# Strassen's seven products for the first expert product of four batches, with its sums on GpSimd

## The chip, the cores and the metric

The kernel runs on one core of a Trainium2 chip. The metric is the device time of one execution in microseconds (us), as the median of several runs. The engines are TensorE (PE, matrix products; its weight loads are listed as PEld), VectorE (DVE), ScalarE (ACT), GpSimd (POOL) and SyncE (SP, which here issues loads). Each engine has its own list of instructions and works it off in order; semaphores hold an instruction until what it needs is there. SBUF is the on-chip memory, PSUM the eight banks that TensorE writes; one bank holds 128 x 512 fp32 values.

## The reference

What is computed, cut to what matters here. A cross-attention between `x` (8 batches, 8 heads, 512 tokens of 64) and 32 states a head gives 4352 rows of 512; then each row goes to the one expert of eight that its gate picks.

```python
scores = scale * np.matmul(x, state.transpose(0, 1, 3, 2))      # softmax -> a
xread  = np.matmul(a, state)                                    # 512 rows per batch
scores2 = scale * np.matmul(state, x.transpose(0, 1, 3, 2))     # softmax -> a2
sread  = np.matmul(a2, x)                                       # 32 rows per batch
x = concatenate([xread, sread], axis=2) -> (B*S, H*D)           # 4352 x 512
logits = x @ w_gate                                             # 8 experts
for e in range(E):
    mask = argmax(logits, 1) == e
    h  = np.maximum(x[mask] @ w1[e], 0.0)                       # 512 -> 1024
    out[mask] = gate_w[mask, None] * (h @ w2[e])                # 1024 -> 512
```

The kernel does not form `xread` for the 512 token rows of a batch. As `xread = a @ state`, it multiplies the states with `w1` once (`G`, 256 x 1024) and then takes `h = relu(G^T a)`, with an inner length of 256 in place of 512. Everything is fp32.

## The kernel before

Per batch b the main part runs two products, both on TensorE. `up` is the first: eight blocks of 128 hidden units, each two matmuls of 128 x 128 by 512 columns into one bank, then a relu on ScalarE into `hT`.

```python
def new_hT():
    return [ffn.tile([128, S], FP32, tag="hT", bufs=NFC, name="hT") for _ in range(NFC)]   # NFC = 8

def up(G, a, hT, i=ALL, insert=None, every=2):
    n = i.stop - i.start
    for f in range(NFC):
        ph = bank("ph")[:, 0:128 * n]
        for g in range(2):
            pe.matmul(ph, lhsT=G[:, g, ts(f, 128)], rhs=a[:, i, g, :], start=(g == 0), stop=(g == 1))
        relu(hT[f][:]..., ph...)
        if insert and f % every == every - 1:
            next(insert, None)                 # a slot: other work is put in here
    return hT
```

The second product is plain (`down`) for batches 0 to 2. For batches 3 to 7 it already goes by Strassen's halves in Winograd's form: seven products of halves in place of eight. The products are named `pX`, `pD`, `pX` again (added onto the first), `pY`, `pZ`, `pW`, `pD` again; each is eight matmuls of 256 columns. The sums of activations (`Sa`, `Sb`) are made on VectorE, those of weights (`Ta`, `Tb`) on GpSimd, and results are combined in `yh` by VectorE.

```python
def down_by_halves(b, hT, w2t, insert, between):
    ...
    Sa, Sb, Ta, Tb = (new(t) for t in ("Sa", "Sb", "Ta", "Tb"))
    for f in range(4):
        dve.tensor_tensor(Sa[:, f], A(1, 0, f), A(1, 1, f), ALU.add)
    gp.tensor_tensor(Ta[:], W(0, 1), W(0, 0), ALU.subtract)
    ...
    pX = new_bank("pX")
    product(pX, lambda f: A(0, 0, f), W(0, 0))
    ...
    done()                                     # between(n), a slot, between(n) again
    pD = new_bank("pD")
    product(pD, lambda f: Sa[:, f], Ta)
    ... (pX again, pY, pZ, pW: as above)
    product(pD, lambda f: Sa[:, f], W(1, 1), start=False)
    store(yB, 1, 0)
    add(yA, pD, yA, 0)
    store(yA, 0, 1)                            # stores are issued by ScalarE
    done()
```

Between the products 3 and 4 the next batch's `G` is made (`pG`, copied out by ScalarE). Into the slots goes first the attention of later batches, then the rounds: the state rows (256 in all) are sorted by expert into groups of 32, four groups a round, three rounds. One round is `ptx` (transposes), four jobs `pgh` (a quarter of the first product), `pth` (transposes), four jobs `pgy` (a quarter of the second). Its weights come in tiles `s` of 1 MB, each as four loads, four tiles for the first product and three for the second. A `yield` ends the work of one slot; two in a row leave a slot empty.

```python
def rounds(r0, r1):
    ...
    round_experts(r0)
    fetch(2, 0)
    yield
    yield
    round_in(r0)                               # load of xg
    fetch(S1B - 2, S2B)
    for _ in range(6):
        yield
    for r in range(r0, r1):
        round_x(r)                             # ptx
        ...
        for k in range(NDC):
            round_up(r, k)                     # pgh
            fetch(2, 0)
            yield
            if k < NDC - 1 and r + 1 < r1:
                yield
        round_relu(r)
        yield
        round_h(r)                             # pth
        yield
        for f in range(0, NFC, 2):
            for i in range(2):
                round_down(r, f + i)           # pgy
                fetch(0, 1)
            if f + 2 == NFC:
                round_out(r)
            yield
            if r + 1 < r1:
                yield
```

The first product of batch b + 1 follows the second of batch b. PSUM has four banks in turn for all these products, two more (`t`) for `ptx`, `pth` and `pG`, and two (`g`) for `pgh` and `pgy`.

Of the kernel before, what the change touches and what calls it, by code (L numbers as in the profile page):

```python
# [9 lines left out]
FP32 = mybir.dt.float32  # L10
# [3 lines left out]
ALU = mybir.AluOpType  # L14
# [6 lines left out]
def kernel(  # L21
# [34 lines left out]
    B, H, S, D = x.shape  # L56
# [497 lines left out]
    def relu(dst, src):  # L554
        act.activation(dst, src, AF.Relu)
# [14 lines left out]
        return G  # L570

    def new_hT():
        return [ffn.tile([128, S], FP32, tag="hT", bufs=NFC, name="hT") for _ in range(NFC)]

    def up(G, a, hT, i=ALL, insert=None, every=2):

        n = i.stop - i.start
        for f in range(NFC):
            ph = bank("ph")[:, 0:128 * n]
            for g in range(2):  # L580
                pe.matmul(ph, lhsT=G[:, g, ts(f, 128)], rhs=a[:, i, g, :], start=(g == 0), stop=(g == 1))
            relu(hT[f][:].rearrange("p (c i t) -> p i c t", c=NC, i=4)[:, i],
                 ph.rearrange("p (i c t) -> p i c t", i=n, c=NC))
            if insert and f % every == every - 1:
                next(insert, None)
        return hT

    def down(hT, w2t, store, insert=None, between=None):
        for c in range(NC):
            py = bank("py")  # L590
            for f in range(NFC):
                pe.matmul(py[:], lhsT=hT[f][:, ts(c, 128)], rhs=w2t[:, f, :],
                          start=(f == 0), stop=(f == NFC - 1))
                if insert and f == 3:
                    next(insert, None)
            store(c, py)
            if insert:
                step = between(c)
                next(step)
                next(insert, None)  # L600
                next(step)

    def down_by_halves(b, hT, w2t, insert, between):


        def A(i, j, f):
            return hT[4 * j + f][:, ts(i, 256)]

        def W(j, k):
            return w2t[:, ts(j, 4), ts(k, 256)]  # L610

        def new(tag):
            return late["sst"].tile([128, 4, 256], FP32, tag=tag, name=tag)

        Sa, Sb, Ta, Tb = (new(t) for t in ("Sa", "Sb", "Ta", "Tb"))
        for f in range(4):
            dve.tensor_tensor(Sa[:, f], A(1, 0, f), A(1, 1, f), ALU.add)
        gp.tensor_tensor(Ta[:], W(0, 1), W(0, 0), ALU.subtract)
        for f in range(4):
            dve.tensor_tensor(Sb[:, f], A(0, 0, f), A(1, 0, f), ALU.subtract)  # L620
        gp.tensor_tensor(Tb[:], W(1, 1), W(0, 1), ALU.subtract)
        g = [gw[:, NC * b + c, :] for c in range(NC)]
        rows = out[ds(b * SO, S)].rearrange("(p c) f -> p c f", c=NC)
        n = [0]

        def product(to, a, w, start=True, stop=True):
            for c in range(2):
                for f in range(4):
                    pe.matmul(to[:, c], lhsT=a(f)[:, ts(c, 128)], rhs=w[:, f], start=(start and c == f == 0),
                              stop=(stop and f == 3), skip_group_check=True)  # L630
            n[0] += 1

        def done():
            step = between(n[0])
            next(step)
            next(insert, None)
            next(step)

        def new_bank(name):
            return bank(name)[:].rearrange("p (c d) -> p c d", c=2)  # L640

        def new_y():
            return ffn.tile([128, 2, 256], FP32, tag="y", bufs=YB, name="yh")

        def store(y, i, k):
            no_dep(act.dma_start(out=rows[:, ts(i, 2), ts(k, 256)], in_=y[:]))

        def add(y, p, u, i):
            for c in range(2):
                dve.scalar_tensor_tensor(y[:, c], p[:, c], g[2 * i + c], u[:, c], ALU.mult, ALU.add)  # L650

        pX = new_bank("pX")
        product(pX, lambda f: A(0, 0, f), W(0, 0))
        yA, yB = new_y(), new_y()
        for i, y in enumerate((yA, yB)):
            for c in range(2):
                act.activation(y[:, c], pX[:, c], AF.Copy, scale=g[2 * i + c])
        done()
        pD = new_bank("pD")
        product(pD, lambda f: Sa[:, f], Ta)  # L660
        for f in range(4):
            dve.tensor_tensor(Sa[:, f], Sa[:, f], A(0, 0, f), ALU.subtract)
        gp.tensor_tensor(Ta[:], W(1, 1), Ta[:], ALU.subtract)
        done()
        product(pX, lambda f: A(0, 1, f), W(1, 0), start=False)
        yC = new_y()
        for c in range(2):
            act.activation(yC[:, c], pX[:, c], AF.Copy, scale=g[c])
        store(yC, 0, 0)
        done()  # L670
        pY = new_bank("pY")
        product(pY, lambda f: Sa[:, f], Ta)
        add(yA, pY, yA, 0)
        add(yB, pY, yB, 1)
        for f in range(4):
            dve.tensor_tensor(Sa[:, f], A(0, 1, f), Sa[:, f], ALU.subtract)
        gp.tensor_tensor(Ta[:], W(1, 0), Ta[:], ALU.subtract)
        done()
        pZ = new_bank("pZ")
        product(pZ, lambda f: Sb[:, f], Tb)  # L680
        add(yB, pZ, yB, 1)
        yD = new_y()
        add(yD, pD, yB, 1)
        done()
        pW = new_bank("pW")
        product(pW, lambda f: A(1, 1, f), Ta)
        store(yD, 1, 1)
        add(yB, pW, yB, 1)
# [4 lines that stand above are left out]
        store(yA, 0, 1)  # L693
        done()
# [175 lines left out]
    def rounds(r0, r1):  # L870
        need1.extend((r, k, half) for r in range(r0, r1) for k in range(NDC) for half in range(2))
        need2.extend((r, f) for r in range(r0, r1) for f in range(NFC))
# [3 lines that stand above are left out]
        yield  # L876
        round_in(r0)
        fetch(S1B - 2, S2B)
        for _ in range(6):
            yield  # L880
        for r in range(r0, r1):
            round_x(r)
            if r + 1 < r1:
                round_experts(r + 1)
                round_in(r + 1)
            yield
            for k in range(NDC):
                round_up(r, k)
# [6 lines that stand above are left out]
            round_h(r)  # L895
# [3 lines that stand above are left out]
                    round_down(r, f + i)  # L899
                    fetch(0, 1)  # L900
                if f + 2 == NFC:
                    round_out(r)
                yield
                if r + 1 < r1:
                    yield


    early, lazy = [], []
    begin()

    def first():
# [45 lines left out]
    def batch(b):  # L957

        nonlocal G, hT

        def between(c):
            nonlocal G
            if c == (1 if b else 2) and b + 1 < B:
                G = states_w1(new_G(), w1s[b + 1], stG[:, b + 1])
            yield
            if c == 1 and 0 < b < B - 2:
                lazy.extend(w1_parts(b + 2, expert_of(eb, b + 2)))
            yield

        def between_products(n):  # L970
            nonlocal G
            if n in (3, 4) and b + 1 < B:
                if n == 3:
                    G = new_G()
                states_w1(G, w1s[b + 1], stG[:, b + 1], (n - 3,),
                          lambda name: late["ps_t"].tile([128, 512], FP32, tag="t", bufs=2, name=name))
            yield
            if n == 4 and b + 2 < B:
                lazy.extend(w1_parts(b + 2, expert_of(eb, b + 2)))
            yield  # L980

        if b < NE:
            down(hT, w2s[b], store_batch(b), slots, between)
        else:
            down_by_halves(b, hT, w2s[b], slots, between_products)
        if 0 < b < B - 2:
            lazy.extend(w2_parts(b + 2, expert_of(eb, b + 2)))
        if b + 1 < B:
            hT = up(G, aT[b + 1], new_hT(), insert=slots)
        if b == 0:  # L990
            e2 = expert_of(eb, 2)
            lazy.extend(w1_parts(2, e2) + w2_parts(2, e2))
# [126 lines left out]
```

## Time and profile before

| | before |
|---|---|
| median of three runs | 463.08 us (462.61 to 463.59) |
| span of the profiled execution | 460.7 us |
| DMA, whole span | 110.04 MB, mean 239 GB/s |
| first product of the batch 4, 5 or 6 (`ph` x32 with its slots) | from 245.5, 296.8 and 347.7 us |

The profile is one execution. In its slices, groups and chain every instruction is named by engine, operation and tile, for instance `ph<-aTl,G` for a matmul that reads `aTl` and `G` and writes `ph`. Each fp32 matmul appears as two records. Nearly all instructions stand at line L48, which is a helper that records them, so one goes by the tiles' names. The attention and batches 0 to 2 fill the time to about 200 us; batch 3's first product follows from 199.9 us, and from there on each batch takes about 51 us.

### The profile page before, as it was taken

Reading aid. Unit: us, or ns where it says so; the run is one execution under the profiler, and the core shown is the slowest. Engines: PE = TensorE matmul, PEld = TensorE weight load, DVE = VectorE, ACT = ScalarE, POOL = GpSimd, SP = SyncE. Lnnn points to the kernel's source line nnn. Section 1 sums busy time; section 2 is a strip of 40 time slices with the busy share of each in tenths; the row PEclk is TensorE's granted clock in tenths of the full one; section 3 lists DMA queues with packets and bytes.
Section 4 is the critical chain, followed back from the end, with each engine's and each line's share of the span. In section 5 each row is a group of like instructions: output and inputs, shape, how many; then the busy total and the mean of one; then the engine's idle time right before and its main releaser. Section 6 shows DMA issues by size and latency. Waiting matters only on the chain.

```text
span 460.7 us, 9525 instructions
## 1 busy us (share of the span) xinstructions
PE 442.5 (96%) x3713; PEld 252.7 (55%) x3713; DVE 177.4 (39%) x445; ACT 119.2 (26%) x266; POOL 87.7 (19%) x76
## 2 busy tenths in 40 slices
PE   3899999999999999999999999999999999999995
PEld 3575545454545544446674475636674466636652
DVE  4838662738275552233240224104131215102231
ACT  1333233533323433223212231022203220123100
POOL 2011040322121230023322022031331022400300
PEclk9999999999999999999999999999999999999999
DMA  6980588315675632539999976999869986690492
GB/s 194 340 283 2 179 272 295 124 55 183 249 221 213 213 112 98 167 90 346 377 306 381 384 285 206 328 340 402 290 203 365 390 284 208 243 334 30 123 367 72
DMA packets 68402, 110.04 MB, mean 239 GB/s; under 512 B 12927, under 2 KB 27263, under 8 KB 68352
## 3 DMA queue, kind: packets, MB, share of 16 engines
q1 hardware_dynamic: 60096, 99.86, 63.7%
q10 hardware_dynamic: 7856, 8.47, 5.2%
q0 software_dynamic: 400, 1.05, 0.6%
q8 instruction: 31, 0.51, 0.5%
q14 instruction: 19, 0.16, 0.1%
HBM read 94.15 MB, written 14.95 MB: 237 GB/s over the span
## 4 chain that ended last, share of the span: by engine, by line
PE 82%; DVE 10%; DMA 3%; ACT 2%; issue 1%; SPq 1%; POOL 1%; ACTq 0%; POOLq 0%; DVEq 0%
PE ph L48 20%; PE py L48 12%; PE pD L48 8%; PE pX L48 8%; PE pgy L48 5%; PE pgh L48 5%; PE pW L48 4%; PE pY L48 4%; PE pZ L48 4%; PE pc L48 4%; PE pG L48 3%; DVE xt L48 3%; DVE sm L48 1%; PE pt L48 1%; DVE nm L48 1%; DMA w1t<-in_moe_w_dram 1%
## 5 line engine op out<-in xcount | busy, mean ns | idle before, releaser
L48 PE MATMUL py<-w2t,hT 128*128 128x512 f32 x192 | 87.5, 601 | 0.0
L48 PE MATMUL ph<-aTl,G 128*128 128x512 f32 x160 | 71.6, 599 | 0.0
L48 ACT ACTIVATE hT<-ph 128x512 f32<-128x512 f32 (+1 forms) x72 | 39.2, 550 | 123.2 <-PE ph L48 123.0
L48 PEld LDWEIGHTS py<-w2t,hT 128*128 128x128 f32 x192 | 34.7, 190 | 39.2 <-issue 38.7
L48 PEld LDWEIGHTS ph<-aTl,G 128*128 128x128 f32 x160 | 29.4, 190 | 40.1 <-issue 39.2
L48 POOL TENSOR_TENSOR Ta<-w2t,Ta 128x1024 f32<-128x1024 f32 x10 | 24.9, 2486 | 135.1 <-PE pD L48 99.2
L48 PE MATMUL ph<-aTe,G 128*128 128x256 f32 (+1 forms) x128 | 44.0, 493 | 0.5 <-DVE aTe L48 0.5
L48 PE MATMUL pX<-w2t,hT 128*128 128x256 f32 x160 | 36.4, 380 | 0.0
L48 PEld LDWEIGHTS pX<-w2t,hT 128*128 128x128 f32 x160 | 30.0, 190 | 6.4 <-issue 2.6
L48 PEld LDWEIGHTS ph<-aTe,G 128*128 128x128 f32 x128 | 23.3, 190 | 15.7 <-issue 12.9
L48 DVE TENSOR_TENSOR Sa<-hT 128x256 f32<-128x256 f32 x20 | 9.7, 503 | 49.3 <-ACT hT L48 49.3
L48 DVE SCALAR_TENSOR_TENSOR yh<-pY,gw,yh 128x256 f32<-128x256 f32 x20 | 8.3, 476 | 45.5 <-PE pY L48 45.5
L48 PE MATMUL pgy<-s,shT 128*32 128x512 f32 x192 | 25.6, 599 | 0.0
L48 ACT ACTIVATE yh<-pX,gw 128x256 f32<-128x256 f32 x30 | 12.0, 473 | 44.7 <-PE pX L48 41.8
L48 POOL TENSOR_TENSOR sx<-sx,mx 128x1024 f32<-128x1024 f32 x6 | 11.5, 1912 | 63.5 <-DVE mx L48 63.5
L48 PE MATMUL pgh<-s,sxT 128*32 128x512 f32 x192 | 23.1, 598 | 0.0
L48 ACT COPY G<-pG 128x512 f32<-128x512 f32 x32 | 16.8, 593 | 24.3 <-PE pG L48 24.3
L48 PE MATMUL pc<-xt,stT 32*32 32x128 f32 x1024 | 18.3, 295 | 3.9 <-DVE xt L48 3.9
L48 DVE STREAM_TRANSPOSE sx<-pc 128x256 f32<-128x256 f32 x32 | 11.6, 418 | 23.8 <-PE pc L48 23.8
L48 PE MATMUL pG<-w1t,stG 64*32 64x512 f32 x256 | 19.0, 605 | 1.1 <-DMA w1t<-in_moe_w_dram 1.1
L48 ACT ACTIVATE y<-py,gw 128x512 f32<-128x512 f32 x12 | 8.3, 688 | 44.3 <-PE py L48 44.3
L48 PE MATMUL pW<-Ta,hT 128*128 128x256 f32 x80 | 18.6, 386 | 0.0
(157 smaller groups left out, 510.4 us busy)
## 6 DMA issues: line engine op xcount, KB each, us to landing
s<-in_moe_w_dram SPq DMA_DIRECT2D x192, 256.0 KB, 5.1
w2t<-in_moe_w_dram SPq DMA_DIRECT2D x32, 512.0 KB, 6.5
w1t<-in_moe_w_dram SPq DMA_DIRECT2D x28, 512.0 KB, 6.1
x_nat<-in_x_dram SPq DMA_DIRECT2D x16, 512.0 KB, 5.7
out_dram<-yh ACTq DMA_DIRECT2D x20, 256.0 KB, 3.8
out_dram<-y ACTq DMA_DIRECT2D x12, 256.0 KB, 2.4
at_dram<-aTl SPq DMA_DIRECT2D x5, 512.0 KB, 3.9
w1t<-in_moe_w_dram SPq DMA_DIRECT2D x2, 1024.0 KB, 6.2
```

What stands on the lines that cost most here:

```text
L48: ins = getattr(self.engine, name)(*args, **kw)
```

## The change

The first product of batches 4 to 7 is made by Strassen's halves too: `G` and `a` are split into quarters, and seven products of quarters (128 inner, 512 hidden, 256 tokens) take the place of eight. It is for taking matmul work off TensorE. The sums of quarters before the products are made on GpSimd, the combination after them on VectorE, the relu in place on ScalarE. Products 1 and 2, and 5 and "5 again", share a pair of banks by accumulating. For this, `h` is held in four tiles of two chunks each, so that sums and additions take 512 elements in one instruction. The first six sums are issued once `pZ` of the batch before is done; the last two (`last`) after the second product, in the tiles of `Sb` and `Tb`, which the second product shares. In addition the rounds begin two slots sooner (4 in place of 6 empty slots), and the last round has two more empty slots in its second half.

```diff
     def new_hT():
-        return [ffn.tile([128, S], FP32, tag="hT", bufs=NFC, name="hT") for _ in range(NFC)]
+        return [ffn.tile([128, 2, S], FP32, tag="hT", bufs=NFC // 2, name="hT") for _ in range(NFC // 2)]
...
+    def up_sums(G, a):
+        Sx, Tx = new_sums("Sb"), new_sums("Tb")
+        T3 = late["sst"].tile([128, 256], FP32, tag="T3", name="T3")
+        ...
+        gp.tensor_tensor(S1, A(1, 0), A(1, 1), ALU.add)
+        gp.tensor_tensor(v(T1), B(0, 1), B(0, 0), ALU.subtract)
+        gp.tensor_tensor(S2, S1, A(0, 0), ALU.subtract)
+        gp.tensor_tensor(v(T2), B(1, 1), v(T1), ALU.subtract)
+        gp.tensor_tensor(S3, A(0, 0), A(1, 0), ALU.subtract)
+        gp.tensor_tensor(v(T3), B(1, 1), B(0, 1), ALU.subtract)
+        def last():
+            gp.tensor_tensor(v(T2), B(1, 0), v(T2), ALU.subtract)
+            gp.tensor_tensor(S2, A(0, 1), S2, ALU.subtract)
+        return S1, S2, S3, T1, T2, T3, last
+
+    def up_by_halves(G, a, sums, hT, insert):
+        ...
+        def product(to, A, B, start=True, stop=True):
+            for f in range(4):
+                pe.matmul(to[f // 2][:, f % 2], lhsT=A[:, ts(f, 128)], rhs=B, ...)
+        def add(i, j, p, u=None):
+            for k in range(2):
+                dve.tensor_tensor(H(i, j, k), p[k], H(*(u or (i, j)), k), ALU.add)
+        def positive(i, j, p=None):
+            for k in range(2):
+                relu(H(i, j, k), p[k] if p else H(i, j, k))
+
+        odd, even = pair("ph6"), pair("ph1")
+        product(even, G_block(G, 0, 0), a_block(a, 0, 0), stop=False)
+        for k in range(2):
+            act.copy(H(0, 1, k), even[k])
+        product(odd, S2, T2)
+        add(0, 1, odd)
+        last()
+        next(insert, None)
+        product(even, G_block(G, 0, 1), a_block(a, 1, 0), start=False)
+        positive(0, 0, even)
+        odd = pair("ph7")
+        product(odd, S3, T3)
+        add(1, 0, odd, (0, 1))
+        next(insert, None)
+        even = pair("ph5")
+        product(even, S1, T1, stop=False)
+        add(1, 1, even, (1, 0))
+        positive(1, 1)
+        next(insert, None)
+        odd = pair("ph4")
+        product(odd, G_block(G, 1, 1), T2)
+        add(1, 0, odd)
+        positive(1, 0)
+        product(even, S2, a_block(a, 1, 1), start=False)
+        add(0, 1, even)
+        positive(0, 1)
+        pair("skip")
+        next(insert, None)
+        return hT
...
-        for f in range(4):
-            dve.tensor_tensor(Sa[:, f], A(1, 0, f), A(1, 1, f), ALU.add)
+        sums(Sa, lambda k: A2(1, 0, k), lambda k: A2(1, 1, k), ALU.add)      # two of 512 elements; Sb and the later Sa likewise
...
-        for _ in range(6):
+        for _ in range(4):
             yield
...
-                if r + 1 < r1:
+                if r + 1 < r1 or f < 4:
                     yield
...
+            if n == 5 and b + 1 < B:
+                sums_of[b + 1] = up_sums(G, aT[b + 1])
...
-        if b + 1 < B:
+        if b + 1 in sums_of:
+            hT = up_by_halves(G, aT[b + 1], sums_of[b + 1], new_hT(), slots)
+        elif b + 1 < B:
             hT = up(G, aT[b + 1], new_hT(), insert=slots)
```

`a_block` reads the tokens of a quarter in runs of 32 columns (`"p i (c t) -> p c i t"`), where the old product read runs of 128.

More of the change, by code (lines that the diff above doesn't have):

```diff
@@ L581, in up @@
                 pe.matmul(ph, lhsT=G[:, g, ts(f, 128)], rhs=a[:, i, g, :], start=(g == 0), stop=(g == 1))
-            relu(hT[f][:].rearrange("p (c i t) -> p i c t", c=NC, i=4)[:, i],
+            relu(hT[f // 2][:, f % 2].rearrange("p (c i t) -> p i c t", c=NC, i=4)[:, i],
                  ph.rearrange("p (i c t) -> p i c t", i=n, c=NC))
@@ L585, in up, with new_sums, G_block, a_block @@
                 next(insert, None)
+        return hT
+    def new_sums(tag):
+        return late["sst"].tile([128, 4, 256], FP32, tag=tag, name=tag)
+    def G_block(G, i, k):
+        return G[:, k, ts(i ^ 1, 512)]
+    def a_block(a, k, j):
+        return a[:, :, k, ts(j ^ 1, 64)].rearrange("p i (c t) -> p c i t", c=2)
+    def up_sums(G, a):
+        Sx, Tx = new_sums("Sb"), new_sums("Tb")
+        T3 = late["sst"].tile([128, 256], FP32, tag="T3", name="T3")
+        S1, S2 = (Sx[:, ts(k, 2)].rearrange("p u t -> p (u t)") for k in range(2))
+        S3 = Tx[:, 0:2].rearrange("p u t -> p (u t)")
+        T1, T2, T3 = Tx[:, 2], Tx[:, 3], T3[:]
+        def A(i, k):
+            return G_block(G, i, k)
+        def B(k, j):
+            return a_block(a, k, j)
+        def v(t):
+            return t.rearrange("p (c i t) -> p c i t", c=2, i=4)
+        gp.tensor_tensor(S1, A(1, 0), A(1, 1), ALU.add)
[8 more added lines that the diff above has]
+        return S1, S2, S3, T1, T2, T3, last
@@ new lines, in up_by_halves, with H, pair @@
+    def up_by_halves(G, a, sums, hT, insert):
+        S1, S2, S3, T1, T2, T3, last = sums
+        def H(i, j, k):
+            return hT[2 * (i ^ 1) + k][:, :, ts(j ^ 1, 256)]
+        def pair(name):
+            return [bank(name)[:].rearrange("p (f t) -> p f t", f=2) for _ in range(2)]
+        def product(to, A, B, start=True, stop=True):
+            for f in range(4):
+                pe.matmul(to[f // 2][:, f % 2], lhsT=A[:, ts(f, 128)], rhs=B, start=(start and f % 2 == 0), stop=stop,
+                          skip_group_check=True)
+        def add(i, j, p, u=None):
[32 more added lines that the diff above has]
+        next(insert, None)
@@ L591, in down @@
             for f in range(NFC):
-                pe.matmul(py[:], lhsT=hT[f][:, ts(c, 128)], rhs=w2t[:, f, :],
+                pe.matmul(py[:], lhsT=hT[f // 2][:, f % 2, ts(c, 128)], rhs=w2t[:, f, :],
                           start=(f == 0), stop=(f == NFC - 1))
@@ L606, in A, with A2, sums @@
         def A(i, j, f):
-            return hT[4 * j + f][:, ts(i, 256)]
+            return hT[2 * j + f // 2][:, f % 2, ts(i, 256)]
+        def A2(i, j, k):
+            return hT[2 * j + k][:, :, ts(i, 256)]
         def W(j, k):
             return w2t[:, ts(j, 4), ts(k, 256)]
-        def new(tag):
-            return late["sst"].tile([128, 4, 256], FP32, tag=tag, name=tag)
-        Sa, Sb, Ta, Tb = (new(t) for t in ("Sa", "Sb", "Ta", "Tb"))
-        for f in range(4):
-            dve.tensor_tensor(Sa[:, f], A(1, 0, f), A(1, 1, f), ALU.add)
+        def sums(to, a, b, op):
+            for k in range(2):
+                dve.tensor_tensor(to[:, ts(k, 2)], a(k), b(k), op)
+        Sa, Sb, Ta, Tb = (new_sums(t) for t in ("Sa", "Sb", "Ta", "Tb"))
+        sums(Sa, lambda k: A2(1, 0, k), lambda k: A2(1, 1, k), ALU.add)
         gp.tensor_tensor(Ta[:], W(0, 1), W(0, 0), ALU.subtract)
-        for f in range(4):
-            dve.tensor_tensor(Sb[:, f], A(0, 0, f), A(1, 0, f), ALU.subtract)
+        sums(Sb, lambda k: A2(0, 0, k), lambda k: A2(1, 0, k), ALU.subtract)
         gp.tensor_tensor(Tb[:], W(1, 1), W(0, 1), ALU.subtract)
@@ L660, in down_by_halves @@
         product(pD, lambda f: Sa[:, f], Ta)
-        for f in range(4):
-            dve.tensor_tensor(Sa[:, f], Sa[:, f], A(0, 0, f), ALU.subtract)
+        sums(Sa, lambda k: Sa[:, ts(k, 2)], lambda k: A2(0, 0, k), ALU.subtract)
         gp.tensor_tensor(Ta[:], W(1, 1), Ta[:], ALU.subtract)
@@ L674, in down_by_halves @@
         add(yB, pY, yB, 1)
-        for f in range(4):
-            dve.tensor_tensor(Sa[:, f], A(0, 1, f), Sa[:, f], ALU.subtract)
+        sums(Sa, lambda k: A2(0, 1, k), lambda k: Sa[:, ts(k, 2)], ALU.subtract)
         gp.tensor_tensor(Ta[:], W(1, 0), Ta[:], ALU.subtract)
@@ L903, in rounds @@
                 yield
-                if r + 1 < r1:
+                if r + 1 < r1 or f < 4:
                     yield
-    early, lazy = [], []
+    early, lazy, sums_of = [], [], {}
     begin()
```

## The prediction

> **What bounds the kernel now.** I read the page's busy shares first, then the chain of waits from 280 us to the end in order of time, then the groups by form from 240 us on, and last the timelines of TensorE, GpSimd and the load queue.
>
> ```profile
> PE 442.5 (96%) x3713; PEld 252.7 (55%) x3713; DVE 177.4 (39%) x445; ACT 119.2 (26%) x266; POOL 87.7 (19%) x76
> PE 82%; DVE 10%; DMA 3%; ACT 2%; issue 1%; SPq 1%; POOL 1%; ACTq 0%; POOLq 0%; DVEq 0%
> ```
>
> TensorE is busy 96% of the span. Busy shares alone do not show that its work sets the end; the chain does. Its columns are start, length, what, and number of records:
>
> ```profile
> 296.85 7.07 PE ph L48 x16
> 303.91 1.85 PE pgy L48 x16
> 305.76 7.06 PE ph L48 x16
> 312.83 0.44 PE ptx L48 x4
> 313.26 3.46 PE pX L48 x16
> 316.72 1.85 PE pgh L48 x16
> 318.57 3.65 PE pD L48 x16
> ...
> 432.58 3.65 PE pY L48 x16
> 436.23 3.12 PE pgy L48 x16
> 439.35 3.65 PE pZ L48 x16
> 443.00 2.14 PE pgy L48 x16
> 445.14 3.65 PE pW L48 x16
> 448.80 2.77 PE pgy L48 x16
> ```
>
> From 280 to 455 us the chain holds nothing but TensorE, back to back, so each us taken from its stream there is a us of the kernel. Every matmul is two records, so `ph` x16 is eight matmuls of 512 columns. Three prices come from these lines. (1) A 512-column record costs 0.43 us (3.44 us for eight without a weight load laid bare). (2) A 256-column record costs 3.45/16 = 0.2156 us, exactly half: narrow matmuls carry no penalty here. (3) The first matmul after a 32-column job (`pgh`, `pgy`, `pG`) shows 0.19 us more (3.65 against 3.46), one weight load. The last three `pgy` take 3.12, 2.14 and 2.77 us in place of 1.85: 2.48 us of waiting for weights. One more gap stands at the first `ptx`:
>
> ```profile
> 230.65 0.66 PE L48 MATMUL ptx<-ident,xg 128*128 128x128 f32 x4 [0.73 <-ACT G L48]
> 213.00 0.33 SPq L48 DMA_DIRECT2D xg<-ss_dram  x1
> ```
>
> It waits 0.73 us for the PSUM tiles that `G` is still being copied from. Its input was asked for at 213.00.
>
> **What the Trainium skill says.** "TensorE: Matmul & The Clock Gate", section "Wait — 56ns, not 53.3ns?", gives a start-to-start time of columns divided by 2.4 GHz plus about 2.5 ns. The trace agrees in form: 215.6 ns for 256 fp32 columns is two array cycles a column and about 2 ns, and halving the width halves the time. "GPSIMD Engine Reference", "Performance versus the Vector engine", gives 4497 ns for a two-input add of 2048 fp32 and calls VectorE 1.96 times faster; the trace has 2402 ns for 1024. "SBUF — State Buffer", section "SBUF: two separate sides", makes VectorE operations with two SBUF inputs block against GpSimd. The trace supports a slowdown: `Sa<-hT,Sa`, which overlaps a GpSimd sum, takes 597 ns, the same size without it 423. So GpSimd pays only where there is time to hide it; below there is.
>
> ```profile
> L48 POOL TENSOR_TENSOR Tb<-w2t 128x1024 f32<-128x1024 f32 x4 | 9.6, 2402 | 0.0
> L48 DVE TENSOR_TENSOR Sa<-hT,Sa 128x256 f32<-128x256 f32 x16 | 8.6, 597 | 0.0
> L48 DVE TENSOR_TENSOR Sa<-hT 128x256 f32<-128x256 f32 x16 | 6.5, 423 | 42.7 <-ACT hT L48 42.7
> L48 DVE SCALAR_TENSOR_TENSOR yh<-pY,gw,yh 128x256 f32<-128x256 f32 x16 | 6.6, 476 | 37.8 <-PE pY L48 37.8
> L48 ACT ACTIVATE hT<-ph 128x512 f32<-128x512 f32 x32 | 19.1, 597 | 89.4 <-PE ph L48 89.2
> ```
>
> **The change part by part.**
>
> *TensorE.* For each of the batches 4 to 7 the product `ph` was 16 matmuls of 512 columns: 32 records × 0.43 = 13.76 us. It becomes seven products of four matmuls of 256 columns: 56 × 0.2156 = 12.07 us. That is 1.69 us a batch, 6.75 us in all. Both forms have four slots in which other work is interleaved, and the 30 jobs of the three rounds stay, so the bared weight loads of price (3) stay too.
>
> *GpSimd, new.* Eight sums a batch, four of 512 elements and four of 256, at 2402/1024 = 2.35 ns each element: 4 × 1.20 + 4 × 0.60 = 7.2 us. The first four (3.6 us) must end before the second product, `ph6`. They start when `pZ` ends. Between lie at least `pW` 3.65, `pD` 3.45, `ph1` 1.73 and one or two jobs of the rounds: 9 us or more, against 3.6 (5.4 for all six of the first group). The last two sums (1.8 us) start after `ph6`; `ph4` needs the first of them 5.2 us later, and the last product needs the second 6.9 us later. `Ta` (2.4 us) follows, and `Tb` waits for `ph4`; both are ready before `pD` and `pZ` of the next stage. All hidden.
>
> *VectorE, new.* Ten additions of a 128x512 PSUM tile a batch. The 128x512 copy out of PSUM on this engine (`shT`) takes 0.69 us, so I estimate 0.7 us each: 7 us in a stage of 12 us and slots. Followed through the order in which the kernel is built, with ph1 starting at 0 and no slot filled: `ph6` ends at 3.45, its two additions at 4.2 against 5.2 when `ph7` wants the banks; `ph7` ends 6.9, its additions 7.7 against 8.6 (`ph4`); `ph5` ends 8.6, its additions 9.4 against 10.35 (last product). The chain of tiles has about 1 us of slack at each step.
>
> *ScalarE.* Ten copies and relus of 0.6 us in place of eight. `ph1`'s copies end at 2.4 against 3.45. Where no slot lies between `pD` and `ph1`, ScalarE is held about 1.4 us by the three stores of the stage before, and the copies end near 3.2. Hidden.
>
> *h in tiles of two.* VectorE's sums in the second product halve in number and double in size; the same elements, a few tenths saved off the path. The first sum of batch 3 now starts after the last relu instead of beside the product; `pD` wants it 3.5 us later, after `pX`. No effect.
>
> *Rounds two slots sooner.* In the new order `ptx` follows the first `pD` (near 220.6 us) and leaves the PSUM tiles well before `pG`: the gap of 0.73 us goes. The two slots come back in the last round, where its `pgy` jobs, until now 5.5 us apart, get 7 to 9 us for the first gaps. Only the final one keeps 5.5. Of the 2.48 us of waits I take back 1.9 and leave 0.6.
>
> Sum: 6.75 + 0.73 + 1.9 = 9.4 us; 463.1 − 9.4 = 453.7. I add 0.3 for small waits at the new tile boundaries: **454.0 us**.
>
> **Rivals.** *The loads become the bound early in the rounds.* The queue issues 20 quarters in a row:
>
> ```profile
> 213.53 14.33 SPq L48 DMA_DIRECT2D s<-in_moe_w_dram  x20
> 228.16 3.23 SPq L48 DMA_DIRECT2D w2t<-in_moe_w_dram  x3
> 235.84 6.04 SPq L48 DMA_DIRECT2D s<-in_moe_w_dram  x8
> ```
>
> Between 210 and 265 us the load engines are full (the table of stretches gives 371, 332 and 385 GB/s). The third weight pair of round 0 is then wanted near 244.8 instead of 252.6. Against that, in the new order it is released near 227 instead of 235.8, its issue can begin near 232 and would end near 237.7; with 5.7 us to landing that is 243.4, one us in hand. If that us is not there, 1 to 3 us are lost: 455 to 457. *A sum arrives late.* If GpSimd's 32-element runs or its blocking against VectorE made each sum twice as slow, the first four would still fit, but a tile boundary inside the stage could cost about 0.5 us, eight to twelve times: 457 to 460. The slack above speaks against it, and the new additions read one input from PSUM. *The moving operand in runs of 32 columns is read slower.* The old product read runs of 128. Three of the seven products are concerned; at 20% slower that is 3 × 1.73 × 0.2 × 4 = 4 us, so 458. No view of the kernel before shows such a read on the whole array. *TensorE waits at the end anyway,* because the last loads come no sooner: then only 7.5 us remain, 455.6.
>
> **Range and chances.** The saving on TensorE is arithmetic with measured prices and the chain shows the end following it; what is open is almost all on the slow side (loads at the start, the end's waits). 8 in 10: 452.8 to 457.0 us. The 2% line is 453.8, just below my figure, so: faster 0.44, within 2% 0.53, slower 0.03.
>
> **What would show it.** The groups `ph1`, `ph4` to `ph7` should have 224 records at a pitch of 0.216 us, and each stage of seven products should add 12.1 us to the chain; if those products show over 1.73 us apiece, the read or the sums are slow. GpSimd's new sums should end some us before `ph6`, and the chain should hold no VectorE, ScalarE or GpSimd piece before 445 us. The first `ptx` should have no idle time. The last four `pgy` should be 1.85 us save the final one. I am wrong if `pgh` of round 0 shows waits for `s`, or if the new products stand in the chain behind a sum, an addition or a copy.

## The result and the profile after

| | before | changed |
|---|---|---|
| median | 463.19 us (462.61 to 463.76, 6 runs) | 456.08 us (454.71 to 458.40, 6 runs) |
| ratio, 95% interval | | 0.9849 (0.9821 to 0.9876) |
| span of the profiled execution | 460.7 us | 456.4 us |

The change takes 1.5% off. Its runs lie 3.7 us apart, those of before 1.2 us; the execution that was profiled is the slowest of the six. The busy shares of the changed kernel, from its page:

```profile
PE 439.4 (96%) x3809; PEld 271.5 (59%) x3809; DVE 198.5 (43%) x445; ACT 124.3 (27%) x274; POOL 120.1 (26%) x108
```

TensorE lost only 3.1 us of busy time, GpSimd gained 32 and VectorE 21. The busy share hides short waits (in the table of stretches further down, 20 us count as fully busy though a job in them waits 1.6 us), so the gain has to be looked for in the chain of waits of the changed kernel, in order of time (start, length, what, records):

```profile
222.11 0.44 PE ptx L48 x4
...
246.16 1.85 PE pgh L48 x16
248.01 7.10 PE ph L48 x32
255.12 1.85 PE pgh L48 x16
256.97 5.38 PE ph L48 x24
...
276.65 3.47 PE pgy L48 x16
280.12 3.65 PE pY L48 x16
...
438.27 1.85 PE pgy L48 x16
440.13 3.65 PE pW L48 x16
443.78 3.54 PE pgy L48 x16
447.32 3.67 PE pD L48 x16
```

The seven products of batch 4 take 7.10 + 5.38 = 12.48 us, of which 0.38 are two weight loads that no other work hides (0.19 us each, as in the prediction's third price): 12.10 us for 56 records, 0.216 us each. They stand back to back; no sum, addition or copy is between them, in this batch or the three later ones. The first `ptx` takes 0.44 us with no gap ahead of it. But two `pgy` jobs stand there with 3.47 and 3.54 us in place of 1.85.

From here on one measure is used for all kernels: the stretch of TensorE from batch 3's first product (`ph` x32, start near 200 us) to the end of the last `pD`, and in it the waits, that is what each `pgh` or `pgy` job takes over 1.85 us, plus the gap at the first `ptx`. Before: 255.3 us, with waits of 2.5 us in the jobs and 0.7 in the gap. Changed: 249.7 us, with waits of 4.4 (1.6 at 276.65, 1.7 at 443.78, the rest in four smaller ones). Without waits this is 252.1 against 245.3: **in the profiled executions TensorE's own work fell by 6.8 us, and 1.2 us of that was given back in waits.** Of the 6.8 us, 0.2 is the first `ptx`, which took 0.66 us behind its gap and takes 0.44 now; 6.6 are the products. As the profiled execution of the changed kernel is the slowest of six, its waits can be larger than usual; the medians further down say how much. It also entered this stretch 1.3 us later than the one before (201.2 against 199.9); a kernel below with the same first 200 us enters it at 198.8, so that difference is not put down to the change.

The load queue of the changed kernel shows where the early wait comes from (start, length of the whole group, what, number of loads).

```profile
259.40 8.21 SPq L48 DMA_DIRECT2D s<-in_moe_w_dram  x8
267.88 1.73 SPq L48 DMA_DIRECT2D w2t<-in_moe_w_dram  x3
270.17 23.47 SPq L48 DMA_DIRECT2D s<-in_moe_w_dram  x24
```

Round 0's fourth tile of second weights belongs to the last line. Its buffer comes free in the `pgy` job at 266.68, but SyncE issues its loads in order and is busy until 269.6 with the next round's first weights (the eight at 259.40, due only at 317) and a weight of batch 5 (due only at 314). Asked for from 270.17 on, it is wanted near 277.6, and the last wait of the job for it ends at 279.1. The load engines are full here: 380 GB/s from 260 to 280 us.

### The profile page after: what moved, and what is told of

It reads as the page before. It is cut to its first block, busy times and chain, and to the rows that moved or that the text cites. A ratio compares the mean times of both kernels' runs of the same rounds, so it can differ in the third digit from the quotient of the medians.

```text
span 456.4 us, 9813 instructions
## 1 busy us (share of the span) xinstructions
PE 439.4 (96%) x3809; PEld 271.5 (59%) x3809; DVE 198.5 (43%) x445; ACT 124.3 (27%) x274; POOL 120.1 (26%) x108
## 4 chain that ended last, share of the span: by engine, by line
PE 79%; DVE 11%; DMA 5%; ACT 1%; issue 1%; SPq 1%; POOL 0%; ACTq 0%; POOLq 0%; DVEq 0%
PE ph L48 19%; PE py L48 11%; PE pD L48 8%; PE pX L48 8%; PE pgy L48 6%; PE pgh L48 5%; PE pY L48 4%; PE pW L48 4%; PE pZ L48 4%; DMA w1t<-in_moe_w_dram 3%; PE pc L48 3%; PE pG L48 3%; DVE xt L48 3%; DVE sm L48 1%; DVE nm L48 1%; PE pw L48 1%
## 5 line engine op out<-in xcount | busy, mean ns | idle before, releaser
L48 POOL TENSOR_TENSOR Ta<-w2t,Ta 128x1024 f32<-128x1024 f32 x10 | 26.1, 2612 | 76.5 <-PE pD L48 45.2
L48 DVE TENSOR_TENSOR hT<-ph,hT 128x512 f32<-128x512 f32 x40 | 27.7, 692 | 37.1 <-PE ph L48 37.1
L48 ACT ACTIVATE hT<-ph 128x512 f32<-128x512 f32 (+1 forms) x48 | 24.9, 528 | 47.4 <-PE ph L48 47.4
L48 PE MATMUL ph<-aTl,G 128*128 128x256 f32 (+1 forms) x96 | 29.6, 456 | 0.0
L48 PE MATMUL pgy<-s,shT 128*32 128x512 f32 x192 | 27.0, 599 | 0.0
L48 PEld LDWEIGHTS ph<-aTl,G 128*128 128x128 f32 x96 | 17.7, 190 | 12.7 <-issue 11.4
L48 PE MATMUL pG<-w1t,stG 64*32 64x512 f32 x256 | 20.8, 629 | 0.8 <-DMA w1t<-in_moe_w_dram 0.6
L48 ACT ACTIVATE hT<-hT 128x512 f32<-128x512 f32 x24 | 14.8, 632 | 22.9 <-DVE hT L48 22.9
```

The costliest lines, as they stand in the source:

```text
L48: ins = getattr(self.engine, name)(*args, **kw)
```

## The experiments

My theory, called A in the expectations: the new products cost what they should and everything round them is hidden; what is given back is waiting for the rounds' weights. B: beginning the rounds sooner does the harm. C: the new stage itself loses time through late sums, through blocking between GpSimd and VectorE, or through the additions. All results in one table; "stretch" is the measure above, from one profile each. The kernel before was timed again beside each kernel (medians of 462.82 to 463.19 us), and the ratios are to those times.

| kernel | median us | ratio to before (95%) | stretch | waits in it |
|---|---|---|---|---|
| before | 463.19 | 1 | 255.3 | 3.2 |
| changed | 456.08 | 0.9849 (0.9821 to 0.9876) | 249.7 | 4.4 |
| strassen_only | 457.11 | 0.9873 (0.9853 to 0.9893) | 250.1 | 4.5 |
| rounds_only | 460.58 | 0.9954 (0.9941 to 0.9968) | 253.9 | 2.0 |
| sums_dve | 455.46 | 0.9854 (0.9838 to 0.9869) | 248.6 | 3.3 |
| before_q0 | 460.64 | 0.9953 (0.9936 to 0.9969) | 252.9 | 0.7 |
| after_q0 | 453.85 | 0.9792 (0.9772 to 0.9811) | 245.3 | 0 |
| s2b4 | 456.18 | 0.9863 (0.9848 to 0.9877) | 248.4 | 3.0 |
| defer | 461.81 | 0.9970 (0.9958 to 0.9983) | 255.2 | 9.8 |
| defer_s2b4 | 457.84 | 0.9885 (0.9869 to 0.9900) | 253.5 | 8.1 |
| s2b4_mid | 452.74 | 0.9786 (0.9773 to 0.9800) | 245.5 | 0.2 |
| s2b4_mid5 | 454.63 | 0.9816 (0.9802 to 0.9829) | 247.9 | 2.5 |
| rounds_mid | 459.74 | 0.9925 (0.9911 to 0.9939) | 252.3 | 0.4 |

Read down the table, every stretch less its waits comes to 245.3 to 245.6 us with the new product, and to 251.9 to 252.2 with the old one.

**The two halves of the change alone: strassen_only and rounds_only.**

```diff
 strassen_only, against the changed kernel
-        for _ in range(4):
+        for _ in range(6):
             yield
...
-                if r + 1 < r1 or f < 4:
+                if r + 1 < r1:
                     yield
 rounds_only: the kernel before with the opposite edits of the same two lines
```

> The change without its two edits of the rounds (six empty slots before the first transposes and no empty slots in the last round, as before). Theory A, the loads eat what TensorE gives: the first products still give 6.75 us, the gap of 0.73 us at the first transposes stays, the last pgy jobs stay 5.5 us apart and wait 2.5 to 3.5 us together, and the early pgy of round 0 wait less than the 1.6 us of the changed kernel: 456.0 to 457.5 us, about what the whole change has. Theory B, beginning the rounds sooner is what hurts: this kernel is clearly faster than the changed one, 454.5 us or less. Theory C, the new stage itself loses time (sums, additions): 458 us or more.

> The kernel before with only the two edits of the rounds. Theory A: the gap of 0.73 us goes, the last pgy jobs lose 1 to 2 us of their waits, and little is lost early since the stages are still long: 461.0 to 462.5 us. Theory B (beginning sooner hurts): 463.5 us or more, with waits for s in round 0.

The chain of waits of strassen_only:

```profile
229.59 0.57 ACT G L48
230.17 0.04 issue
230.21 0.65 PE ptx L48 x4
...
405.24 2.81 PE pgh L48 x16
...
430.49 2.33 PE pgy L48 x16
...
436.47 2.50 PE pgy L48 x16
...
442.63 3.23 PE pgy L48 x16
```

The gap behind `G` is still there, the `pgy` jobs of round 0 (not in the lines, as they take 1.85) no longer wait, and the three at the end wait 2.5 us, one `pgh` of the last round 1.0. So without the two edits the early wait is gone and the late ones are back: about the same time. rounds_only gained 2.2 us from the edits, a little more than I had expected; its only large wait is the last `pgy` with 2.0 us. Alone the halves give 5.7 (462.82 less 457.11) and 2.2 us, 7.9 together, and the whole 7.1 (463.19 less 456.08); that difference of 0.8 us lies within the intervals. Theory B falls: the earlier begin helps the old product, and does not hurt the new one by more than it gives.

**sums_dve: the eight sums on VectorE.**

```diff
 in up_sums (eight lines)
-        gp.tensor_tensor(S1, A(1, 0), A(1, 1), ALU.add)
+        dve.tensor_tensor(S1, A(1, 0), A(1, 1), ALU.add)
```

> The changed kernel with the eight sums of each first product on VectorE in place of GpSimd. Theory A: sums are hidden on either engine, so no difference over 0.5 us from the changed kernel: 455.5 to 456.7 us. If GpSimd's sums had cost something through the shared port or by arriving late (theory C): 1 us or more faster. If VectorE's order is too tight for them: slower, with hT or Sa in front of ph or pD in the chain.

455.46 us, a ratio of 0.9854 against 0.9849: no difference that can be told. On either engine the sums are hidden, so theory C is left with the additions.

**before_q0 and after_q0: three of four weight loads of the rounds left out.** Only the first group's weights are loaded, and all four groups of a round multiply with them; the matmuls stay. State rows of the other groups so come out with another expert's product.

```diff
 in round_w1 and round_w2
-        for q in range(4):
+        for q in range(1):
 in round_up and round_down: [:, q, :] of the tile becomes [:, 0, :]
```

> The kernel before with three of four round weight loads left out: all four groups of a round are multiplied with the first group's expert (so state rows of other experts get the wrong expert's result), the matmuls stay. No wait for s is left; the gap at the first transposes stays. TensorE from batch 3's first product to its end: 252 to 253 us in place of 255.3. Time 460 to 461 us.

> The changed kernel with the same three of four loads left out. Theory A, waits for these loads are all that the change gives back: TensorE from batch 3's first product to its end takes 245.3 to 246 us, the time 452 to 453.3 us, 7.2 to 8 us under the kernel before without these loads. Theory C, the new stage costs something of its own: 454 us or more with waits on GpSimd, VectorE or ScalarE in the chain.

This is the cleanest view of the change without the loads: the stretch goes from 252.9 to 245.3 us, 7.5 us (6.6 of products, 0.9 of the gap and the longer first `ptx`), and the medians from 460.64 to 453.85, 6.8 us where 7.2 to 8 were expected. The median of after_q0 is half a us above what I wrote and close to the 454 us of theory C. But its stretch is what theory A expected, and no wait on another engine appears in it, so theory C falls too; its profile enters the stretch at 201.0 us, 1.2 us later than that of before_q0, for a reason that is not known.

The medians also say what the loads cost in a usual execution. Leaving them out takes 0.57% (0.9849 less 0.9792), about 2.6 us, off the changed kernel, and 0.47%, about 2.2 us, off the kernel before. The two differ by less than their intervals. So the 1.2 us given back is what the profiled execution shows; that a usual one gives anything back is not shown, only that the loads still cost it some 2 to 3 us.

**s2b4: a fourth tile for the second weights.**

```diff
-    S1B, S2B = 4, 3
+    S1B, S2B = 4, 4
...
-        xT = late["sst"].tile([128, NDC, 128], FP32, tag="sxT", bufs=2, name="sxT")
+        xT = late["sst"].tile([128, F], FP32, tag="sh", bufs=1, name="sxT")    # its first half is used
```

> The changed kernel with four tiles in place of three for the rounds' second weights (the room comes from letting sxT use the buffer of sh). Theory A: the waits of pgy for s, 4.4 us in the profile of the changed kernel, fall to about 1 us, and the time to 452.5 to 454 us. Theory C or any loss that is not a wait for these weights: 455.5 to 457 us as the changed kernel.

A miss: 456.18 us. The waits of `pgy` did go, but TensorE's timeline has a new one (a row is start, length, what, and in brackets the gap ahead and its cause):

```profile
244.41 2.69 PE L48 MATMUL pgh<-s,sxT 128*32 128x512 f32 x12
247.34 2.02 PE L48 MATMUL pgh<-s,sxT 128*32 128x512 f32 x4 [0.23 <-DMA s<-in_moe_w_dram]
249.29 1.99 PE L48 MATMUL ph<-aTl,G 128*128 128x256 f32 x8
```

The `pgh` job that begins at 244.41 ends at 249.29: 3.0 us too long. The four loads of the new tile were asked for with the other three at the start, ahead of the third pair of first weights, which this job reads. The wait moved from a job that is due at 276 to one that is due at 244.

**defer and defer_s2b4: the next round's weights later.**

```diff
 defer, against the changed kernel (defer_s2b4: against s2b4, and the first four s2 tiles
 only after round 0's third and fourth pgh job)
                 round_up(r, k)
-                fetch(2, 0)
+                if k < 2:
+                    fetch(2, 0)
...
+                if f in (2, 4):
+                    fetch(2, 0)
                 if f + 2 == NFC:
                     round_out(r)
```

> The changed kernel with the first weights of the next round asked for later (after the second and third pgy job in place of after the third and fourth pgh job); TensorE's order and the buffers are the same. Theory A in its stricter form (bandwidth, so the order of the loads decides): the early wait of pgy in round 0, 1.6 us, goes, the one at the very end stays: 454 to 455 us. If it is a lack of buffers rather than of order: 455.5 to 457 us.

> The same later loads with four tiles for the second weights, and round 0's second weights asked for only after its third and fourth pgh job, so that they no longer stand ahead of its third first weights. Theory A: TensorE runs without waits for s, 245.3 to 246.3 us, and the time is 452.3 to 453.5 us, better than both kernels. If bandwidth itself is short over the whole stretch: waits only move, 455 us or more.

Both misses, the first the largest of the study: 461.81 and 457.84 us. The early wait of `pgy` went as expected, but I had taken the queue's fullness for a lack that holds only there. A stretch of the load engines in the changed kernel, and the same stretch in defer (the last two columns are the share of the load engines and GB/s):

```profile
260.00:280.00 20.00, 20.00 (x115) 12.96 (x114) 6.95 (x11) 7.47 (x16) 5.25 (x2) 1.00 1.04 380
```

```profile
260.00:280.00 20.00, 20.00 (x123) 14.00 (x122) 5.77 (x9) 6.07 (x13) 4.63 (x2) 1.00 0.58 193
```

The loads put off are missing from this stretch, and they are made up later, where they stand ahead of others: by the order of issue in the kernel, the eight loads of a pair of round 2, due only at 394.9, go ahead of the tile that the job below waits for. TensorE's timeline of defer a hundred us on:

```profile
374.76 1.06 PE L48 MATMUL pgy<-s,shT 128*32 128x512 f32 x8
378.22 4.46 PE L48 MATMUL pgy<-s,shT 128*32 128x512 f32 x8 [2.39 <-DMA s<-in_moe_w_dram]
382.62 3.80 PE L48 MATMUL pY<-Ta,Sa 128*128 128x256 f32 x16
```

One `pgy` job lasts from 374.76 to 382.62, 6.0 us over its 1.85. So loading ahead in a full queue was not the fault; it kept the later stretches free.

**s2b4_mid and s2b4_mid5: the fourth tile at another place.** What these runs suggest: keep the order of all loads, and put just the one extra tile where it stands ahead of something that is due late, but behind what is due soon.

```diff
 s2b4_mid, against s2b4
-        fetch(S1B - 2, S2B)
+        fetch(S1B - 2, S2B - 1)
...
                 round_up(r, k)
+                if r == r0 and k == 2:
+                    fetch(0, 1)
                 fetch(2, 0)
 s2b4_mid5: besides, range(5) for the empty slots at the start and f < 2 for those in the last round
```

> The changed kernel with four tiles for the second weights; the loads keep their order, except that the fourth tile is asked for after round 0's third pgh job, ahead of the next round's first weights. Theory A, waits are a matter of which load stands ahead of which in a queue that is full from 212 to 280 us: neither pgh nor pgy of round 0 waits, the end waits under 0.7 us, TensorE takes 245.5 to 247 us from batch 3's first product to its end, time 452.7 to 454.3 us. If a load brought forward always takes its time from another that is due (as the fourth tile at the start did): 455.5 us or more, with the wait at another job.

> The same with the rounds begun one slot sooner than before in place of two, and one empty slot in the last round in place of two. Theory A: a slot more for the early loads and one less for the last; with four tiles the end does not need the second: 452.7 to 454.5 us. If the end still lives on latency: waits of 1 to 2 us at the last pgy jobs, 454.5 to 456 us.

s2b4_mid takes 452.74 us, 0.9786 of before (0.9773 to 0.9800): better than both kernels. Its chain of waits, at the places shown for the changed kernel:

```profile
220.15 0.44 PE ptx L48 x4
...
244.19 1.85 PE pgh L48 x16
246.05 7.10 PE ph L48 x32
...
274.69 1.85 PE pgy L48 x16
...
433.78 1.85 PE pgy L48 x16
435.63 3.65 PE pW L48 x16
439.28 1.85 PE pgy L48 x16
441.14 3.67 PE pD L48 x16
```

No job waits for more than 0.13 us. Its five runs lie 1.0 us apart where those of the changed kernel lie 3.7 apart. s2b4_mid5 stands 1.9 us behind, and not through its end, as its rival expectation had it: its last `pgy` do not wait. The first `ptx` falls back between `pG` and `pY`, into the PSUM tiles that `G` is copied from, as this row of its TensorE timeline shows:

```profile
227.51 0.66 PE L48 MATMUL ptx<-ident,xg 128*128 128x128 f32 x4 [1.87 <-ACT G L48]
```

The wait is 1.9 us here and was 0.7 before; the chain puts ahead of this `G` copy a store of ScalarE that was held until loads had landed at 226.4. (This profile is the slowest of its five runs, so the typical wait is shorter.) With the 0.2 us by which `ptx` itself is longer, this is 2.1 of the 2.4 us by which its stretch exceeds that of s2b4_mid. So in these profiles most of what the second slot is worth lies in the place of `ptx`, ahead of `pG`.

**rounds_mid: the old product with the same rounds and the same fourth tile.**

> The kernel before with the two edits of the rounds and the fourth tile placed as in s2b4_mid, but with the old first product (the short stages are not in it). Theory A: TensorE takes 252.1 to 252.6 us from batch 3's first product to its end, 6.6 to 6.8 more than s2b4_mid, and the time is 458.8 to 460 us. If the fourth tile and not the short stages made s2b4_mid fast: under 457 us.

459.74 us; its stretch of 252.3 us is 6.7 us longer than that of s2b4_mid, 6.6 without the waits of both. The fourth tile, the earlier rounds and the two empty slots of the last round give the old product 3.1 us (462.83 less 459.74), and the new product gives its 6.6 to 7.0 us on top (459.74 less 452.74 is 7.0).

## Why the prediction was right, and where it was not

The time lies in the range; the single figure was 2.1 us too low.

*Products: right.* 6.75 us were foretold from the price of a 256-column record. Where the rounds stand alike, the stretches less their waits give 6.6 (strassen_only against before, the changed kernel against rounds_only, s2b4_mid against rounds_mid). The reads in runs of 32 columns have no price of their own: `ph<-aTl,Sb` reads `a` in such runs, `ph<-Tb,Sb` reads a tile without them, and both take the same time on TensorE, so that rival is out:

```profile
249.77 1.89 PE L48 MATMUL ph<-Tb,Sb 128*128 128x256 f32 x8
260.46 1.89 PE L48 MATMUL ph<-aTl,Sb 128*128 128x256 f32 x8
```

Nor was the 0.3 us that I added for tile boundaries needed: batch 4 took 12.10 us against 12.07.

*Sums: right.* The instructions of GpSimd in the changed kernel, by form:

```profile
L48 POOL TENSOR_TENSOR Tb<-aTl,Tb 128x256 f32<-128x256 f32 x8 | 5.8, 727 | 26.9 <-PE ph L48 26.9
L48 POOL TENSOR_TENSOR Sb<-G 128x512 f32<-128x512 f32 x4 | 5.1, 1280 | 9.0 <-issue 6.8 <-PE pZ L48 2.3
```

1.27 to 1.28 us for 512 elements and 0.73 for 256, against 1.20 and 0.60 in the sum: 8.0 us a batch in place of 7.2. The timeline of GpSimd in batch 4 shows the first six done at 243.1, where `ph6` begins at 249.77, and the last two at 253.8, where `ph4` begins at 258.73:

```profile
242.40 0.72 POOL L48 TENSOR_TENSOR T<-aTl 128x256 f32<-128x256 f32 x1
251.81 0.73 POOL L48 TENSOR_TENSOR Tb<-aTl,Tb 128x256 f32<-128x256 f32 x1 [8.69 <-PE ph L48]
252.50 1.27 POOL L48 TENSOR_TENSOR Sb<-G,Sb 128x512 f32<-128x512 f32 x1
```

*Additions and copies: right.* 0.69 us each, 0.7 foretold. The timeline of VectorE for `ph6` in the same batch:

```profile
250.91 0.69 DVE L48 TENSOR_TENSOR hT<-ph,hT 128x512 f32<-128x512 f32 x1 [3.83 <-PE ph L48]
251.77 0.69 DVE L48 TENSOR_TENSOR hT<-ph,hT 128x512 f32<-128x512 f32 x1 [0.17 <-PE ph L48]
```

They end at 252.46; `ph7`, which needs the banks, begins at 253.23. That is 0.8 us of slack, where the working had 1.0.

*Gap at the first `ptx`: right.* It is gone, and it is back in s2b4_mid5 and strassen_only, where `ptx` stands behind `pG`. The place was worth 0.2 us more than the gap of 0.73, as `ptx` itself got shorter.

*Waits at the end: this step failed.* "Of the 2.48 us of waits I take back 1.9 and leave 0.6" was mis-sized. The waits for `s` in the profile of the changed kernel are 4.4 us: 1.7 at the very last `pgy`, where I left 0.6, and 2.7 elsewhere that I put at nothing. From the medians with and without these loads I estimate about 2.6 us for a usual execution; that is 2.0 above the 0.6, as much as the 2.1 us by which the single figure was too low, though the intervals leave more than 1 us of play. The end: three tiles and 5.5 us between the last two jobs; the last tile can be asked for only when the job before frees its buffer, and with more empty slots ahead of it the same last gap cost 1.7 and, in rounds_only, 2.0 us. A fourth tile ends it (s2b4_mid). The early part: the rival "the loads become the bound early in the rounds" was the right mechanism at the wrong job. I followed the third pair of first weights, which landed in time, and did not follow the queue further, to the fourth tile of second weights, asked for behind loads that were due 36 us later and more. With 4.4 in place of 0.6, and the products and the place of `ptx` as measured, the sum gives 5.6 us for the stretch, which is what it measures (255.3 less 249.7). The rival that TensorE waits at the end anyway, with 455.6 us, came nearest in number, in part by luck: it put all of the waiting at the end, where the profile has 1.7 of the 4.4 us.

*Not settled:* why the stretch begins between 198.8 and 201.2 us. In the changed kernel's chain a weight of batch 2 (`w1t`) takes 9.1 us to land, where the median of such loads on its page is 6.4. The products `pG` that need it end at 126.1 us there and at 123.7 in sums_dve, so all of the 2.4 us between these two kernels is there by then. Starts at both ends of that range occur with the new form of `h`, and 199.0 to 200.0 with the old; what sets it was not tried.

## What to carry to other kernels

Where the chain is one engine back to back, price the new work by records of that engine and trust the sum; then look for what the shorter stage takes from the loads, job by job along the in-order queue, until the next stretch with free bandwidth. A load is late because of what stands ahead of it: adding a buffer at the front of a full queue moved the wait (456.2 us) and putting other loads off made a longer one later (461.8 us), while one tile placed between due-soon and due-late took it away (452.7 us). The spread of the runs is no sure sign of such waits: it was 3.7 us in the changed kernel and 1.0 in s2b4_mid, but also only 1.1 in s2b4, whose profile has 3.0 us of waits.

## What the runs showed of the hardware that was not expected

In the changed kernel `Sa<-hT,Sa`, a VectorE sum of two SBUF inputs, was slow only where it began while a GpSimd sum was running:

```profile
L48 DVE TENSOR_TENSOR Sa<-hT,Sa x10: 678/1042/1441, 234.2 to 437.8; 128x512 f32<-128x512 f32 x10
```

The three figures are the least, the median and the most in ns. They mix two kinds: five cases that began 1.5 us into the sum `Ta<-w2t,Ta` of GpSimd took 1403 to 1441 ns, and five without a GpSimd instruction beside them 678 to 680. (The 597 ns that the prediction read for `Sa<-hT,Sa` is such a mixed mean too: in the kernel before the five cases beside GpSimd took 1146 to 1162 ns, the others 410 to 414.) `Sa<-Sa,hT`, also with two SBUF inputs, took 691 to 694 ns in all ten cases. In five of them `Ta<-w2t,Ta` began 0.11 us after it, and then it was the GpSimd sum that took longer: 2816 to 2861 ns, against 2376 to 2415 in the five other cases. So here the one that began second was held up.

The new additions, with one input in PSUM, took 691 to 693 ns in all 40 cases, though GpSimd was busy beside 20 of them for most of their time. This agrees with the Trainium skill, "SBUF — State Buffer", section "SBUF: two separate sides", which names two SBUF inputs as the condition. So additions out of PSUM could be put beside GpSimd's sums here at no cost.

GpSimd's sums come to about 0.16 us apiece on top of 2.2 ns an element (worked out from the 1280 ns for 512 elements here and the 2402 ns for 1024 that the prediction shows). For 256 elements this gives 719 ns, and 727 were measured; so the short ones were a fifth dearer than a price per element had them.
